# Batch 0's q in two parts, w_in ahead of batch 1's k, and new lists for sorted block attention with an FFN

## The chip, the cores and the metric

The kernel runs on one core of a Trainium2 chip. The metric is device time in microseconds (us) of one execution; three runs of the kernel before gave a median of 237.82 us (237.7 to 238.86). The trace of a profiled execution gives the span from the first to the last record, 236.6 us here.

## The reference

Batches B=4, heads H=8, tokens S=768, head size D=64. In each head the tokens form 8 blocks of 96. k and v are mixed over blocks by an 8x8 matrix P made from sort_net; the attention then runs inside each block; the heads are joined to x (3072 tokens by 512), and an FFN with a leaky activation (a slope per column) follows.

```
P = sort_net
for _ in range(5):
    P = exp(P - max(P, axis=-1))
    P = P / (sum(P, axis=-1) + 1e-9)
    P = P / (sum(P, axis=-2) + 1e-9)
k_sorted = einsum('bhij,bhjcd->bhicd', P, k_b)      # blocks of 96 tokens
v_sorted = einsum('bhij,bhjcd->bhicd', P, v_b)
scores = (q_b @ k_sorted^T) / sqrt(D)               # 96x96 per block and head
attn = softmax(scores)
x = (attn @ v_sorted) -> (3072, 512)
h = x @ w_in                                        # 512 -> 2048
g = max(h, 0) + alpha * min(h, 0)
out = g @ w_out                                     # 2048 -> 512
```

Inputs and output are fp32; the kernel works in bf16 with fp32 sums.

## The kernel before

The program builds a list of operations with G.add(engines, function, duration, reads, writes, priority). Which engine an operation runs on, and in what order each engine's operations stand, comes from the table SEQ: 1221 operation numbers, a suffix p, a or d choosing POOL, ACT or DVE where several are allowed. The table WARM puts filler matmuls (L808, on the identity) behind given operations. Waits on semaphores are derived from the reads and writes. The durations in the calls are for the planner that searched the table; with the table given they set nothing. An engine runs its list in order, so an operation that waits holds back all behind it.

The 3072 tokens form 32 groups of 96 (group g belongs to batch g // 8). Attention goes group by group, the FFN runs behind it in chunks of groups.

*Loads.* POOL issues all loads that turn fp32 into bf16, in one queue: batch 0's q (L397, into the tile hT that later holds the activations), its k and v (L419, KS0 and VST0), batch 1's k (L419, KS1), w_in in four parts (L908), w_out in two halves (L913), v of batches 1 to 3 in two or four parts (L435), and q of batches 1 to 3 as eight loads, one per head (L401, into QN). SP issues the turning DMAs (transposes), and the output stores (L877).

*q.* TensorE needs q with D on the partitions. Batch 0's q is turned on TensorE: prep_q (L600) multiplies it by the identity in six units of 8 token columns, and ACT copies each to QTz. q of the later batches is turned by six DMA transposes QTz<-QN (L409, turn_q), one per 128 tokens; the first of them reads what all eight loads bring. QTz has two buffers, batches taking turns.

*k and v.* Batch 0: prep_k (L600) multiplies KS by a block diagonal BDK made from P; conv_v (L653) rearranges v, and prep_v (L674) multiplies it. Later batches: conv_k (L616) spreads k into KSz, prep_k (L629) multiplies by BDM; conv_v (L658) spreads v into VDz, prep_v (L669) multiplies by BDV. Copies L372 bring the products to KT and VS.

*Attention of a group.* Scores S1 (L715 in batch 0, L712 later) go to PSUM; DVE takes the negated maximum (L721). In batch 0 a second pass on TensorE makes the turned scores with the maximum added (L736 and L727), and ACT takes the exp (L759) into ET. Later ACT takes the exp (L748) into Esb, and SP turns it (L753) into ET. L768 multiplies ET with VS; DVE normalises (L776, L779) into xq; xq is turned into xT by TensorE (L794, batches 0 and 1) or by a DMA (L787).

*FFN.* L823 multiplies w_in and xT for one of 16 column tiles, ACT (L833) and DVE (L836) apply the activation into hT, and L863 multiplies hT with w_out; L372 copies the result to outstg and L877 stores it. The ops of the FFN are spread between the attention's by the table.

PE, DVE, ACT, POOL and SP thus each follow a fixed list. In the start the order of POOL's list sets the order in which the loads arrive.

## Time and profile before

| | before |
|---|---|
| median of three runs | 237.82 us |
| span of the profiled execution | 236.6 us |
| PE (TensorE matmul) busy | 229.2 us (97%) |
| DVE busy | 169.8 us (72%) |
| ACT busy | 151.6 us (64%) |
| POOL busy | 73.0 us (31%) |
| DMA moved | 31.36 MB, mean 133 GB/s |

Busy times are sums over the instructions of an engine; the matmuls' ends are modelled and a filler matmul counts as busy, so 97% does not mean that TensorE did useful work for so long. In the lists of instructions, L12 is a line of the kernel, "out<-in" its tiles, and the part after a stroke the idle time of the engine before them and what ended it. For a DMA the time to landing is counted from its issue; loads issued by POOL are worked off in their order, so that a long time to landing is mostly waiting behind the loads ahead. The chain of waits follows the end of the program back to what released each step.

### The profile page before, as it was taken

The page shows a single profiled execution, that of the slowest core. Times are in us where ns is not written, and L with a number is a line of the kernel's source. Part 1 is how long each engine was busy: PE and PEld are TensorE (multiplying, and loading weights), DVE is VectorE, ACT ScalarE, POOL GpSimd, SP SyncE. Part 2 cuts the span into 40 slices and gives each one's busy share as a digit, 9 for nine tenths or more (in the row PEclk, how much of TensorE's full clock was granted, in tenths as well). Part 3 has the DMA queues.
Part 4 walks back from the last instruction along what each step waited for, and adds up shares of the span by engine and source line. Part 5 has one row for each costly group of instructions (what it writes and reads, how often), then busy time and mean ns, then how long its engine had stood idle before and what let it go on. Part 6 is the DMA issues. An engine that isn't in the chain of part 4 may idle for free.

```text
span 236.6 us, 6266 instructions
## 1 busy us (share of the span) xinstructions
PE 229.2 (97%) x2532; PEld 142.2 (60%) x2532; DVE 169.8 (72%) x354; ACT 151.6 (64%) x423; POOL 73.0 (31%) x139
## 2 busy tenths in 40 slices
PE   7998998999999999999999999999999999999995
PEld 3446676687666666556566665655555555555543
DVE  4748796989899997868887667676766587744350
ACT  4475265587887988886678786756864646453332
POOL 7958812915659620338590020000000000000000
PEclk9999999999999999999999999999999999999999
DMA  5999999999989999899998796542642323400033
GB/s 96 212 213 168 211 217 202 179 209 158 191 88 167 152 120 173 119 210 166 165 111 114 188 164 135 98 90 52 125 92 82 97 50 79 140 0 1 0 133 135
DMA packets 71453, 31.36 MB, mean 133 GB/s; under 512 B 64504, under 2 KB 65280, under 8 KB 71424
## 3 DMA queue, kind: packets, MB, share of 16 engines
q0 software_dynamic: 22896, 13.63, 42.0%
q1 hardware_dynamic: 48528, 17.33, 37.8%
q8 instruction: 20, 0.33, 0.5%
q14 instruction: 9, 0.07, 0.1%
HBM read 27.28 MB, written 6.29 MB: 142 GB/s over the span
## 4 chain that ended last, share of the span: by engine, by line
PE 76%; DMA 17%; POOL 6%; issue 1%; ACT 0%; POOLq 0%
PE psH L823 31%; PE psYP L863 28%; DMA w_out_bf<-in_moe_w_out_dram 10%; PE psS L863 3%; PE psS L712 3%; DMA VST<-in_v_dram 3%; PE psO L768 3%; PE psYP L669 2%; DMA ET<-Esb 2%; PE psYP L629 1%; DMA QTz<-QN 1%; POOL w_in_bf L908 1%; PE psO L863 1%; PE psS L727 1%; POOL VDz L456 1%; PE psO L794 1%
## 5 line engine op out<-in xcount | busy, mean ns | idle before, releaser
L836 DVE SCALAR_TENSOR_TENSOR hT<-t,omaT,psH 128x384 bf16<-128x384 f32 (+1 forms) x139 | 77.4, 571 | 36.6 <-ACT t L833 35.1
L823 PE MATMUL psH<-xT,w_in_bf 128*128 128x384 bf16 (+1 forms) x556 | 96.9, 311 | 0.0
L833 ACT ACTIVATE t<-psH 128x384 f32<-128x384 f32 (+1 forms) x139 | 63.1, 461 | 50.3 <-PE psH L823 49.2
L863 PE MATMUL psYP<-w_out_bf,hT 128*128 128x512 bf16 x336 | 83.2, 379 | 1.3 <-DMA w_out_bf<-in_moe_w_out_dram 1.3
L823 PEld LDWEIGHTS psH<-xT,w_in_bf 128*128 128x128 bf16 x556 | 49.5, 98 | 28.9 <-DVE hT L836 1.6
L863 PEld LDWEIGHTS psYP<-w_out_bf,hT 128*128 128x128 bf16 x336 | 30.8, 98 | 30.1 <-DMA w_out_bf<-in_moe_w_out_dram 1.8
L748 ACT ACTIVATE Esb<-psS,nf 96x96 bf16<-96x96 f32 x192 | 46.1, 345 | 2.0 <-DVE nf L721 2.0
L721 DVE TENSOR_REDUCE nf<-psS 96x8 f32<-96x768 f32 x24 | 22.8, 951 | 6.4 <-PE psS L712 6.0
L658 POOL COPY VDz<-VST 64x192 f32<-64x192 f32 x39 | 20.4, 524 | 20.3 <-DMA VST<-in_v_dram 16.6
L779 DVE TENSOR_TENSOR xq<-psO,rec 96x512 bf16<-96x512 f32 x31 | 21.2, 683 | 0.5
L401 POOL DMA_DIRECT2D QN<-in_q_dram x24 | 19.8, 833 | 3.3 <-DMA QTz<-QN 2.7
L616 POOL COPY KSz<-KS 64x256 f32<-64x256 f32 x28 | 11.1, 397 | 31.6 <-PE psYP L629 19.8
L712 PEld LDWEIGHTS psS<-KT,QTz 128*96 128x96 bf16 x192 | 12.1, 124 | 3.3 <-DMA QTz<-QN 0.2
L768 PEld LDWEIGHTS psO<-VS,ET 112*128 112x128 bf16 x248 | 11.1, 98 | 3.6 <-ACT ET L759 0.2
L808 PE MATMUL psYP<-identb 128*128 128x512 bf16 x40 | 12.8, 453 | 0.4 <-ACT identb L372 0.4
L372 ACT ACTIVATE VS<-psYP 112x512 bf16<-112x512 f32 x15 | 10.3, 687 | 4.2 <-PE psYP L669 2.2
L768 PE MATMUL psO<-VS,ET 112*128 112x65 bf16 x248 | 12.7, 194 | 0.0
L712 PE MATMUL psS<-KT,QTz 128*96 128x96 bf16 x192 | 12.6, 208 | 0.0
L372 ACT ACTIVATE KT<-psYP 128x512 bf16<-128x512 f32 x15 | 9.0, 599 | 2.8 <-PE psYP L629 1.8
L669 PEld LDWEIGHTS psYP<-BDV,VDz 128*128 128x128 bf16 x192 | 8.2, 98 | 2.7 <-POOL VDz L658 0.4
L372 ACT ACTIVATE outstg<-psYP 128x512 f32<-128x512 f32 x13 | 7.7, 604 | 3.2 <-PE psYP L863 3.2
L669 PE MATMUL psYP<-BDV,VDz 128*128 128x64 bf16 x192 | 9.5, 193 | 0.2 <-POOL VDz L658 0.2
(137 smaller groups left out, 198.8 us busy)
## 6 DMA issues: line engine op xcount, KB each, us to landing
out_dram<-outstg SPq DMA_DIRECT2D x23, 256.0 KB, 2.5
KS<-in_k_dram POOLq DMA_DIRECT2D x3, 768.0 KB, 13.3
QN<-in_q_dram POOLq DMA_DIRECT2D x24, 96.0 KB, 4.4
w_in_bf<-in_moe_w_in_dram POOLq DMA_DIRECT2D x4, 512.0 KB, 17.3
w_out_bf<-in_moe_w_out_dram POOLq DMA_DIRECT2D x2, 1024.0 KB, 23.9
VST<-in_v_dram POOLq DMA_DIRECT2D x4, 384.0 KB, 17.6
hT<-in_q_dram POOLq DMA_DIRECT2D x1, 768.0 KB, 7.6
VST<-in_v_dram POOLq DMA_DIRECT2D x1, 768.0 KB, 11.1
```

What stands on the lines that cost most here:

```text
L372: return e.activation(o, i, ACTF.Copy) if e is nc.scalar else e.tensor_copy(o, i)
L658: G.add(SHIFT, lambda e, o2=o2, i2=i2: e.tensor_copy(o2, i2), {"dve": 424, "pool": 525}, r=vst, w=[("VDz", u % VSL, th)], prio=prio)
L669: inst = e.matmul(AP(t, off + dd * 64, [[row, 128], [1, 64]]), AP(VDz, (u % VSL * 4 + dd // 2) * 256 + dd % 2, [[VSL * 1024, 128], [2, 128]]),
L712: inst = e.matmul(o, AP(QTz[n], hp * 3072 + h4 * 768 + i * 96, [[6144, 128], [1, 96]]), AP(KT[n], (h4 * 8 + i) * bk, [[ld, 128], [64, 2], ...
L721: G.add(DVE, lambda e: e.tensor_reduce(AP(nx, 0, [[8, 96], [4, 2], [1, 4]]), AP(psX, 0, [[1024, 96], [512, 2], [96, 4], [1, 96]]), AxisLis ...
L748: inst = e.activation(AP(Esb[me], p * 128, [[1024, 96], [64, 2], [1, 48]]), AP(psX, (p // 4) * 512 + (p % 4) * 96, [[1024, 96], [48, 2], [ ...
L768: inst = e.matmul(AP(psZ, hp * 512 + h4 * 68, [[1024, 128], [1, 65]]), AP(ET[me] if far else ET[m], pos(h4, hp) * 96, [[800, nk], [1, 128] ...
L779: G.add(DVE, lambda e: e.tensor_tensor(out=AP(xq[me], 0, [[512, 96], [256, 2], [64, 4], [1, 64]]), in0=AP(psZ, 0, [[1024, 96], [512, 2], [ ...
L823: inst = e.matmul(AP(pt, poff, [[1024, 128], [1, n]]), AP(w_in_bf, kt * DFF + ft // 2 * 256 + ft % 2, [[KT_TILES * DFF, 128], [2, 128]]), ...
L833: G.add(ACT, lambda e: e.activation(AP(t1[tb], 0, [[384, 128], [1, n]]), AP(pt, poff, [[1024, 128], [1, n]]), ACTF.Relu, scale=-1.0), t_ac ...
L836: G.add(DVE, lambda e: e.scalar_tensor_tensor(out=AP(hT, ft * RING + tok % RING, [[FT_TILES * RING, 128], [1, n]]), in0=AP(t1[tb], 0, [[38 ...
L863: inst = e.matmul(AP(bank[0], bank[1], [[1024, 128], [1, n]]), AP(hT, ft * RING + tok % RING, [[FT_TILES * RING, 128], [1, 128]]), AP(w_ou ...
```

## The change

Batch 0's q now comes as two loads. The first brings tokens 0 to 191 of every head (a quarter, 12 tokens in each partition's row), into hT as before; the second brings tokens 192 to 767 (36 in each partition's row) into KS[1], where batch 1's k goes later. Their source is walked as 8 heads by 16 runs by the run's elements; the load before was walked as 128 rows of 3072 elements. prep_q has seven units instead of six: two of 6 columns on the first part, four of 8 and one of 4 on the second; their copies to QTz may run on ACT or DVE. The scores of groups 0 and 1 need units 0 and 1 only, the later groups of batch 0 units 2 to 6.

The copies of conv_v in batch 0 may run on ACT too. The durations given to the planner are changed in most calls; SEQ and WARM are new. The core of the diff (SEQ, WARM and lines where only a duration changes are left out):

```
     def load_q(b, prio):
         if b == 0:
-            G.add(POOL, lambda e: e.dma_start(AP(hT, 8192, [[HR, 128], [1, 3072]]), AP(q.tensor, 0, [[3072, 128], [1, 3072]])),
-                  load_us, w=[("QS", 0)], prio=prio, dma=(d_q[0], 0))
+            for x, (t, off, n, t0) in enumerate(((hT, 8192, 12, 0), (KS[1], 0, 36, 192))):
+                ld = HR if t is hT else 3072
+                G.add(POOL, lambda e, t=t, off=off, n=n, t0=t0, ld=ld: e.dma_start(
+                    AP(t, off, [[ld, 128], [1, n * D]]),
+                    AP(q.tensor, t0 * D, [[S * D, 8], [n * D, 16], [1, n * D]])),
+                    load_us * n / 48, w=[("QS", x)] + [("KS", 1)] * x, prio=prio, dma=(d_q[x], 0))
             return
...
     def prep_q(u, prio, bank):
         t, off, row, keys = bank
-        G.add(PE, pairs(hT, 8192, u, identb, 0, 128, bank), 372, r=[("QS", 0), "identb"], w=keys, prio=prio)
-        o = AP(QTz[0], 8 * u, [[6144, 128], [96, 32], [48, 2], [1, 8]])
-        i = AP(t, off, [[row, 128], [2, 32], [1, 2], [64, 8]])
-        G.add(ACT, lambda e: copy(e, o, i), t_act(512), r=keys, w=[("Q0", u)], prio=prio)
+        x = u > 1
+        c0, n = ((0, 6), (6, 6), (0, 8), (8, 8), (16, 8), (24, 8), (32, 4))[u]
+        G.add(PE, pairs((hT, KS[1])[x], (8192, 0)[x], c0, identb, 0, 128, bank, n), 254 * n // 8,
+              r=[("QS", x), "identb"] + [("KS", 1)] * x, w=keys, prio=prio)
+        per = 36 if x else 12
+        o = AP(QTz[0], 192 * x + c0, [[6144, 128], [768, 4], [per, 16], [1, n]])
+        i = AP(t, off, [[row, 128], [16, 4], [1, 16], [64, n]])
+        G.add(EITHER, lambda e: copy(e, o, i), {"act": 142 + n * 64 // 1.2, "dve": 155 + n * 64 // .96}, r=keys, w=[("Q0", u)], prio=prio)
...
+            ob = AP(hT, 8 * u * 64, [[HR, 128], [2, 48], [128, 4], [1, 2]])
+            ib = AP(VST[0], 8 * u, [[3072, 128], [64, 48], [2, 4], [1, 2]])
+            G.add(("pool", "dve", "act"), lambda e: copy(e, ob, ib) if e is nc.scalar else e.tensor_copy(o, i),
+                  {"dve": 335, "pool": 530, "act": 490}, r=vst, w=[("VD", u)], prio=prio)
...
-            [("QTzt", n, t) for t in range(6)] + [("Q0", u) for u in range(6)]
+            [("QTzt", n, t) for t in range(6)] + [("Q0", u) for u in ((0, 1) if i < 2 else range(2, 7))]
...
-    for u in range(6):
-        prep_q(u, -50, (BANK_H + BANK_O + BANK_S)[u])
+    for u in range(2):
+        prep_q(u, -50, BANK_H[u])
     for u in range(6):
         prep_k(0, u, -47, BANKS0[(u + 1) % 5])
     for u in range(8):
         conv_v(0, u, -45.5)
     for u in range(8):
         prep_v(0, u, -45, (BANK_O + [BANK_P])[u % 3])
+    for u in range(5):
+        prep_q(u + 2, -44, (BANK_Y, BANK_P)[u % 2])
```

The lines of the changed kernel are 3 to 14 higher for the same operation: L715 is L727 there, L712 L724, L736 L748, L727 L739, L768 L780, L794 L806, L823 L835, L863 L875, L629 L638, L669 L681, L409 L414, L753 L765, L401 L406, L435 L440, L419 L424, L908 L922, L913 L927.

*The first loads.* POOL's list from the first load on, before:

```order
L397 DMA hT<-in_q_dram 128x3072
L443 ISA
L443 AFFINE_SELECT identf<-identf 128x128
L461 MEMSET QN 128x6x32
L456 MEMSET VDz 128x1024
L461 MEMSET QN 128x6x32
L419 DMA KS0<-in_k_dram 128x3072
L456 MEMSET VDz 128x1024
L419 DMA VST0<-in_v_dram 128x3072
L461 MEMSET QN 128x6x32
L419 DMA KS1<-in_k_dram 128x3072
```

The same engine and place in the changed kernel (L400 are the two parts of q; the KS1 of its second row of that line holds q):

```order
L400 DMA hT<-in_q_dram 128x1x768
L448 ISA
L448 AFFINE_SELECT identf<-identf 128x128
L424 DMA VST0<-in_v_dram 128x3072
L466 MEMSET QN 128x6x32
L424 DMA KS0<-in_k_dram 128x3072
L479 MEMSET Esb0 96x16x8
L400 DMA KS1<-in_q_dram 128x1x2304
L922 DMA w_in_bf<-in_moe_w_in_dram 128x2x1024 x3
L664 COPY hT<-VST0 128x48x4 x4
```

v stands ahead of k now, and the larger part of q behind both; w_in follows, and batch 1's k (L424, KS1) comes after all four parts of w_in and ahead of w_out, behind seven v copies.

*PE around the first group on w_out.* PE's list before, the last ten rows up to that group; psS, psH, psYP and psO are PSUM banks:

```order
L715 MATMUL psS<-KT,QTz 96x96 x8
L768 MATMUL psO<-VS,ET 128x65 x8
L823 MATMUL psH<-xT,w_in_bf 128x192 x8
L823 MATMUL psYP<-xT,w_in_bf 128x192 x4
L808 MATMUL psYP<-identb 128x512
L736 MATMUL psS<-QTz,KT 112x96 x8
L727 MATMUL psS<-identb,nm 112x96 x8
L823 MATMUL psYP<-xT,w_in_bf 128x192 x4
L823 MATMUL psH<-xT,w_in_bf 128x192 x8
L863 MATMUL psYP<-w_out_bf,hT 128x512 x4
```

The same place in the changed kernel, again up to the first group on w_out:

```order
L780 MATMUL psO<-VS,ET 128x65 x8
L835 MATMUL psH<-xT,w_in_bf 128x192 x4
L748 MATMUL psS<-QTz,KT 112x96 x8
L739 MATMUL psS<-identb,nm 112x96 x8
L835 MATMUL psH<-xT,w_in_bf 128x192 x4
L638 MATMUL psYP<-BDM,KSz 128x64 x8
L835 MATMUL psH<-xT,w_in_bf 128x192 x4
L806 MATMUL psO<-identb,xq 128x96 x4
L727 MATMUL psS<-KT,QTz 96x96 x8
L875 MATMUL psYP<-w_out_bf,hT 128x512 x4
```

In the changed list 13 FFN groups of w_in (4 matmuls each) stand ahead of that group, before 10; five second passes instead of four; and the first product of batch 1's k (L638) is already among them.

*Batch 2's loads.* POOL's list at the last loads of batch 1's q (into QN) and the first of batch 2, before:

```order
L401 DMA QN<-in_q_dram 128x6x64 x3
L658 COPY VDz<-VST1 64x48x4 x2
L401 DMA QN<-in_q_dram 128x6x64
L435 DMA VST0<-in_v_dram 64x3072
L419 DMA KS0<-in_k_dram 128x3072
```

The same place in the changed kernel:

```order
L670 COPY VDz<-VST1 64x48x4 x3
L406 DMA QN<-in_q_dram 128x6x64
L625 COPY KSz<-KS1 64x8x32
L406 DMA QN<-in_q_dram 128x6x64
L670 COPY VDz<-VST1 64x48x4
L440 DMA VST0<-in_v_dram 64x3072
L670 COPY VDz<-VST1 64x48x4 x4
L440 DMA VST0<-in_v_dram 64x3072
L670 COPY VDz<-VST1 64x48x4 x4
L670 COPY VDz<-VST0 64x48x4 x5
L424 DMA KS0<-in_k_dram 128x3072
```

Batch 2's k (KS0) now follows both halves of its v (VST0) and thirteen copies of v behind the first half, five of them of batch 2's own v. On SP four turns of batch 1's q stand ahead of the first turn of ET, two behind it; before it was five and one.

234 lines of the change are left out of this document (117 added, 117 removed).

## The prediction

> **What bounds the kernel now.** I read the windows view first, cut at the events that matter: the first FFN group (28.71), the first group on w_out (36.40), batch 1's first scores (56.88), batch 2's first scores (97.42) and the end of TensorE (234.20). The columns are the stretch, its length, then busy us (and count) of PE, PEld, DVE, ACT, POOL, the clock, the DMA share and GB/s.
>
> ```profile
> 28.71:36.40 7.69, 6.39 (x96) 5.20 (x91) 6.99 (x19) 4.37 (x12) 1.81 (x3) 1.00 1.13 217
> 36.40:56.88 20.48, 20.44 (x324) 16.16 (x325) 16.68 (x42) 14.10 (x34) 8.53 (x18) 1.00 1.43 193
> 56.88:97.42 40.54, 40.54 (x461) 26.52 (x460) 37.48 (x70) 34.49 (x107) 22.14 (x41) 1.00 1.12 142
> 97.42:234.20 136.78, 136.50 (x1065) 78.94 (x1063) 90.42 (x161) 84.33 (x241) 17.45 (x32) 1.00 0.58 107
> ```
>
> From 36.40 to 234.20 PE stands still for 0.04 + 0.00 + 0.28 = 0.32 us, and the clock is full. So the end is when PE passes some mark, plus the work that its list still holds. Only what stands ahead of that mark can be won. The second view is the chain that ended last, around the first mark:
>
> ```profile
> 12.19 24.17 DMA w_out_bf<-in_moe_w_out_dram
> 36.40 1.04 PE psYP L863 x4
> ```
>
> The first half of w_out lands at 12.19 + 24.17 = 36.36 and PE stood idle for it. The third view asks for the scores of batch 1 (L712), for the turn of batch 1's q on which they rest (L409) and for the last of the eight loads of that q (L401):
>
> ```profile
> L712 PE MATMUL psS<-KT,QTz x8: 206/208/208, 56.9 to 57.2; 128*96 128x96 bf16 x8
> its engine sat idle before it (us, times) until:
>   DMA QTz<-QN: 0.2, 1
> ...
> L409 SPq DMA_TRANSPOSE QTz<-QN x1: 1354/1354/1354, 50.9 to 50.9; - x1
> DMA to landing us min/median/max: 5.8/5.8/5.8
> ...
> L401 POOL DMA_DIRECT2D QN<-in_q_dram x1: 826/826/826, 41.0 to 41.0; - x1
> DMA to landing us min/median/max: 9.9/9.9/9.9
> ```
>
> The last q load lands at 41.0 + 9.9 = 50.9, the first turn starts there and lands at 50.9 + 5.8 = 56.7, and PE reads it at 56.9 after 0.2 us of waiting. That is a second mark, just met before. It is fed by the queue of loads, not by PE: whatever PE gains ahead of it is lost again unless this turn lands earlier too.
>
> **The change part by part.** *The first loads.* All of these stand in one queue:
>
> ```profile
> L397 POOL DMA_DIRECT2D hT<-in_q_dram x1: 687/687/687, 1.3 to 1.3; - x1
> DMA to landing us min/median/max: 7.6/7.6/7.6
> ...
> L419 POOL DMA_DIRECT2D VST<-in_v_dram x1: 536/536/536, 5.5 to 5.5; - x1
> DMA to landing us min/median/max: 11.1/11.1/11.1
> ...
> L419 POOL DMA_DIRECT2D KS<-in_k_dram x1: 548/548/548, 6.2 to 6.2; - x1
> DMA to landing us min/median/max: 14.1/14.1/14.1
> ```
>
> These are batch 0's q and v and batch 1's k; batch 0's k lies between q and v. Landings: q 1.3 + 7.6 = 8.9, v 16.6, batch 1's k 20.3, so one such load costs (20.3 - 8.9)/3 = 3.8 us of queue, and k landed near 12.7. The new order is a quarter of q, v, k, three quarters of q. With 0.95 for the quarter and 2.85 for the rest this gives v at 9.9 (was 16.6), k at 13.7 (was 12.7), the second part of q at 16.5, and w_in one load earlier. K's products may start up to 1.0 later, in a stretch in which PE still spins warm groups. V's copies and products, which had to wait for 16.6, move ahead. What this buys is read off PE's list: ahead of the first w_out group now stand 13 instead of 10 FFN groups, 5 instead of 4 second score passes (L736 and L727), and six more small groups (two L715, two L794, one L768, one L629). Durations from the chain:
>
> ```profile
> 45.31 0.33 PE psH L823 x4
> 43.93 0.34 PE psS L736 x8
> 44.27 0.54 PE psS L727 x8
> 47.02 0.34 PE psYP L629 x8
> ```
>
> 3 x 0.33 + 0.88 = 1.87, and six small ones at 0.17 (half of the nearest row, since these rows overlap) to 0.34 add 1.0 to 2.0; I take 1.2, together 3.1 us. The bytes ahead of w_out's first half are the same as before (batch 1's k only stands behind w_in instead of ahead), so it lands at 36.4 again, and PE reaches it with 3.1 us more behind it, provided DVE delivers: it is at 6.99 of 7.69 there.
>
> *From w_out to batch 1's scores.* Ahead of L712's first group the two lists hold the same FFN, score and k groups. The new one has two v groups and a part of q's turn more and one L768 less, 0.2 us net. So PE would come there at 36.4 + 20.48 - 3.1 + 0.2 = 54.0. The gain could be 2.9 us, if the turn were there.
>
> *The turn of batch 1's q.* Ahead of its last load stand the same bytes, so that lands at 50.9 again. Two of the eight are now issued behind VDz copies that wait for v, which costs nothing while the queue is still at w_out's second half. What changes is behind them:
>
> ```profile
> L435 POOL DMA_DIRECT2D VST<-in_v_dram x1: 557/557/557, 41.8 to 41.8; - x1
> DMA to landing us min/median/max: 10.1/10.1/10.1
> ...
> L419 POOL DMA_DIRECT2D KS<-in_k_dram x1: 609/609/609, 42.4 to 42.4; - x1
> DMA to landing us min/median/max: 13.3/13.3/13.3
> ...
> L409 SPq DMA_TRANSPOSE QTz<-QN x1: 1233/1233/1233, 82.6 to 82.6; - x1
> DMA to landing us min/median/max: 3.8/3.8/3.8
> ```
>
> Before, half of batch 2's v (until 51.9) and batch 2's k (until 55.7) ran beside this turn, and it landed 1.0 after them. That k took 55.7 - 51.9 = 3.8 us, no longer than undisturbed: it was the turn that stood back. Now that k is issued behind batch 2's v copies, after this time; the second half of v stands there instead, half the bytes, and the queue is empty at about 53.8. One us later is 54.8. A turn with an empty queue took 3.8, which would be 54.7. The upper end is no change, 56.7. I take 55.0, so the scores start at 55.2 instead of 56.9: 1.7 us won, and 0.2 for the work already done.
>
> [...]
>
> *The next wait.* SP now issues four turns, then the turn of the first probabilities (ET), then the last two; before, five stood ahead. What is left for it is PE's work between batch 1's first scores and its first L768:
>
> ```profile
> 68.75 0.41 PE L768 MATMUL psO<-VS,ET 112*128 112x65 bf16 x8
> ET<-Esb SPq DMA_TRANSPOSE x24, 3.3
> 58.50 1.92 ACT L748 ACTIVATE Esb<-psS,nf 96x96 bf16<-96x96 f32 x8
> ```
>
> That was 68.75 - 56.9 = 11.9 us for five w_out groups, six wide and three narrow FFN groups, six v, three L712 and one L794: 27,520 columns through PE. The new list has three, three, three, three, two and one there, and one L768: 17,032 columns, or 7.3 us. Scores to exps took 60.4 - 56.9 = 3.5, and ET lands 3.3 later by the median: 6.8 of 7.3. With a turn as slow as q's above (5.8) it is 2.0 short. I take 0.4 lost, nearer the median, and 0.1 for all later waits.
>
> *What costs nothing.* The new durations in the calls only feed a planner; the order comes from the table. "Any engine" for v's copies is not used: the list puts two on DVE and six on POOL, none on ACT. The warm groups fall from 47 to 45, all ahead of 36.4, where w_out sets the time. Cover for the start is the 1.2 us between PE's 54.0 and the turn's 55.2; a start that is later than that costs what is beyond it.
>
> **The sum.** -1.7 - 0.2 + 0.4 + 0.1 = -1.4 us on the span of 236.6, so 235.2. The median of the three runs, 237.82, lies 1.2 above the span, and so I forecast 236.4 (-0.6%).
>
> **Rivals.** R1, *the turn lands no earlier*: other traffic or the transposer itself sets it at 56.5 to 56.7. Then 0.2 to 0.4 is won and 0.1 to 0.4 lost: 237.7. For it: four turns follow each other there in any case. Against: 3.8 with an empty queue.
>
> R2, *q's parts load at half speed*, the rival on the other side. The source of each part is now walked as 8 heads by 16 by a run of tokens, where before it was 128 rows, and if the work is dealt by the 8, half of the DMA engines carry it. If the parts fall on opposite halves, one half is behind by 2 x 0.75 - 1 = 0.5 load = 1.9 us; on the same half by a whole load, 3.8. Every later load is complete only when the slower half is, so w_out, v, and batch 1's turn all slip: 238.3 or 240.2. It decides against the change from a lag of 1.4 on. No row shows a load of that shape; that all loads before have 64 or 128 rows speaks for nothing. [...]
>
> R3, *DVE becomes the bound between the two score marks*. Between L712's first group of batch 1 and that of batch 2 DVE gets two normalisations, two xT copies and four smaller pieces more, and three evacuations fewer.
>
> ```profile
> L779 DVE TENSOR_TENSOR xq<-psO,rec 96x512 bf16<-96x512 f32 x31 | 21.2, 683 | 0.5
> L372 DVE CAST VS<-psYP 112x512 bf16<-112x512 f32 x11 | 7.6, 688 | 0.8 <-PE psYP L669 0.8
> ```
>
> With 0.68 and 0.2 of reciprocal for each normalisation, half an evacuation for an xT copy and 0.25 for a small piece (estimates from these rows), that is 1.76 + 0.69 + 1.0 - 2.06 = +1.4 on 37.48 of 40.54. If its 3.1 us of gaps stay, PE loses 1.4: 237.8. Against: gaps of an engine that waits for PE shrink first.
>
> **How the numbers follow.** Forecast 0.55 (alone 235.2 to 237.2), R1 0.15, R2 0.18 (two thirds of it opposite halves), R3 0.12. A measurement of this kernel tells about 0.5%, 1.2 us, from no change: below 236.6 is faster, above 239.0 slower. Three quarters of the forecast's chance lies below 236.6, 0.41, and 0.01 of the rest: 0.42. Slower: the same halves and the upper part of the opposite ones 0.10, R3 with a further wait 0.05, and 0.02 for the forecast's own tail: 0.17. Same: 0.41. The range of 8 in 10 is 235.0 (turn at 54.5 and no wait for ET) to 239.2 (R2's opposite halves with a wait behind it).
>
> **What would show it.** Right: v lands near 9.9 and k near 13.7; w_out at 36.4 with no PE wait above 0.5; a PE wait of about 1 us for QTz at 55; L768 within 0.5 of its ET; PE solid after. Wrong: q's second part later than 17.5 and w_out at 38 (R2); L712 at 56.7 or later (R1); PE gaps for DVE between L712's marks (R3). If the last q load of batch 1 lands more than 1 us from 50.9, the sum falls with it, either way.

## Result and profile after

The change makes the kernel slower: 251.36 and 252.44 us against a median of 238.34 (237.70 to 238.90) of the kernel before on the same chip, a ratio of 1.058 [1.053, 1.062]. Two further executions at a lower clock (0.967) took 261.1 and 262.0 and are left out of this; the profiles of e2, e3, e6, e8 and e9 below come from such longer executions, which their ratios leave out as well. Forecast were 236.4 and a range of 235.0 to 239.2.

The windows view of the changed kernel, cut at the events of the prediction: the first FFN group, the first group on w_out, batch 1's and batch 2's first scores, the end of TensorE (columns as there). The stretch from 0 to the first FFN group stands ahead of them:

```profile
0.00:34.72 34.72, 27.07 (x609) 17.61 (x610) 19.82 (x67) 13.76 (x28) 17.69 (x37) 0.95 0.87 158
34.72:44.15 9.43, 9.05 (x145) 7.58 (x144) 8.80 (x24) 6.44 (x18) 7.61 (x14) 1.00 1.08 207
44.15:61.00 16.85, 16.57 (x260) 13.31 (x262) 15.88 (x40) 11.36 (x27) 9.75 (x20) 1.00 1.37 147
61.00:102.22 41.22, 40.52 (x461) 26.38 (x469) 38.32 (x77) 34.61 (x108) 18.79 (x35) 1.00 1.11 146
102.22:246.90 144.68, 137.55 (x1033) 78.34 (x1049) 92.06 (x167) 79.25 (x233) 17.01 (x30) 0.99 0.57 103
```

The first FFN group stood at 28.71, now 34.72: 6.0 later. The first w_out group stood at 36.40, now 44.15: 7.8. Batch 1's scores 56.88, now 61.00: 4.1. From there to the end it was 177.3, now 185.9: 8.6 more. So there are two losses, 4.1 ahead of batch 1's scores and 8.6 behind them. In the second PE is busy for 40.52 + 137.55 = 178.07 against 40.54 + 136.50 = 177.04: 1.0 of the 8.6 is more busy time, 7.6 is more standing still.

What PE waited for, from the waits view (us in total, times, longest):

```profile
PE psO L780 <- DMA ET<-Esb: 5.0, 2, 4.7
PE psYP L686 <- issue: 3.3, 1, 3.3
PE psS L901 <- DVE bz L895: 2.3, 1, 2.3
PE psYP L820 <- ACT identb L373: 1.7, 1, 1.7
PE psYP L875 <- ACT outstg L373: 1.0, 1, 1.0
```

The third and fourth lie ahead of 6 us, where before stood 1.2 and 0.4 for the same two. The first two are what the prediction did not have: 3.3 us in which nothing that the profile shows held PE ("issue"), and a wait for a turn of probabilities. PE's timeline shows both places (start, length, what, and in brackets the idle time ahead):

```profile
20.11 0.28 PE L686 MATMUL psYP<-BDK,hT 128*64 128x64 bf16 x5
23.71 0.46 PE L686 MATMUL psYP<-BDK,hT 128*64 128x64 bf16 x11 [3.32 <-issue]
...
61.00 0.56 PE L724 MATMUL psS<-KT,QTz 128*96 128x96 bf16 x8
...
108.76 0.41 PE L780 MATMUL psO<-VS,ET 112*128 112x65 bf16 x8 [4.71 <-DMA ET<-Esb]
```

The first breaks into a group of v's products after its fifth matmul: 5 run, 11 come 3.3 us later, on the same operands. That is no wait for data. Behind each the granted clock was half for 3.4 us (from 23.8 and from 109.1), which two narrow windows show as 0.60 and 0.66 (the last column but two, PEclk):

```profile
24.00:28.00 4.00, 4.00 (x133) 3.61 (x130) 2.25 (x3) 2.13 (x4) 0.00 (x0) 0.60 0.68 129
108.00:113.00 5.00, 4.11 (x26) 2.17 (x28) 2.10 (x6) 1.92 (x9) 2.76 (x6) 0.66 1.14 238
```

In the kernel before PE had pauses of the first kind too, of 0.5 us each:

```profile
16.11 0.28 PE L600 MATMUL psO<-BDK,KS 64*64 64x64 bf16 x6 [0.51 <-issue]
...
22.33 0.71 PE L674 MATMUL psO<-BDK,hT 128*64 128x64 bf16 x32 [0.52 <-issue]
```

### The profile page after: what moved, and what is told of

It reads as the page before. It is cut to its first block, busy times and chain, and to the rows that moved or that the text cites. A ratio compares the mean times of both kernels' runs of the same rounds, so it can differ in the third digit from the quotient of the medians.

```text
span 249.5 us, 6214 instructions
## 1 busy us (share of the span) xinstructions
PE 230.8 (93%) x2500; PEld 143.2 (57%) x2530; DVE 174.9 (70%) x371; ACT 145.7 (58%) x413; POOL 70.8 (28%) x134
## 4 chain that ended last, share of the span: by engine, by line
PE 75%; DMA 11%; DVE 5%; issue 3%; ACT 2%; POOL 1%; SPq 1%; POOLq 0%; ACTq 0%
PE psH L835 28%; PE psYP L875 24%; DMA ET<-Esb 5%; PE psYP L820 4%; PE psS L875 3%; PE psS L724 3%; DMA QN<-in_q_dram 3%; PE psO L780 3%; DMA QTz<-QN 2%; PE psYP L681 2%; DVE hT L848 1%; PE psYP L638 1%; DVE nm L733 1%; PE psO L875 1%; ACT t L845 1%
## 5 line engine op out<-in xcount | busy, mean ns | idle before, releaser
L835 PE MATMUL psH<-xT,w_in_bf 128*128 128x384 bf16 (+1 forms) x556 | 99.1, 312 | 0.3 <-DVE hT L848 0.2
L875 PE MATMUL psYP<-w_out_bf,hT 128*128 128x512 bf16 x308 | 79.9, 382 | 2.7 <-ACT outstg L373 1.0
L835 PEld LDWEIGHTS psH<-xT,w_in_bf 128*128 128x128 bf16 x556 | 48.9, 98 | 30.3 <-DVE hT L848 4.6
L875 PEld LDWEIGHTS psYP<-w_out_bf,hT 128*128 128x128 bf16 x336 | 31.1, 98 | 30.1 <-ACT outstg L373 1.5
L670 POOL COPY VDz<-VST 64x192 f32<-64x192 f32 x34 | 18.0, 529 | 23.5 <-PE psYP L681 12.4
L406 POOL DMA_DIRECT2D QN<-in_q_dram x24 | 19.9, 835 | 1.1 <-issue 0.4
L780 PE MATMUL psO<-VS,ET 112*128 112x65 bf16 x248 | 12.7, 194 | 5.0 <-DMA ET<-Esb 5.0
L780 PEld LDWEIGHTS psO<-VS,ET 112*128 112x128 bf16 x248 | 11.4, 98 | 9.9 <-issue 5.1
L625 POOL COPY KSz<-KS 64x256 f32<-64x256 f32 x26 | 10.4, 400 | 21.6 <-PE psYP L638 17.6
L724 PEld LDWEIGHTS psS<-KT,QTz 128*96 128x96 bf16 x192 | 11.7, 125 | 2.6 <-DMA QTz<-QN 0.3
L820 PE MATMUL psYP<-identb 128*128 128x512 bf16 x39 | 11.3, 450 | 1.7 <-ACT identb L373 1.7
L724 PE MATMUL psS<-KT,QTz 128*96 128x96 bf16 x192 | 12.6, 208 | 0.1
L373 ACT ACTIVATE VS<-psYP 112x512 bf16<-112x512 f32 x13 | 8.9, 687 | 5.1 <-PE psYP L686 3.6
L681 PE MATMUL psYP<-BDV,VDz 128*128 128x64 bf16 x192 | 9.8, 195 | 0.0
L681 PEld LDWEIGHTS psYP<-BDV,VDz 128*128 128x128 bf16 x192 | 8.3, 100 | 2.4 <-POOL VDz L670 0.6
L373 DVE CAST VS<-psYP 112x512 bf16<-112x512 f32 x13 | 8.9, 685 | 0.2
## 6 DMA issues: line engine op xcount, KB each, us to landing
w_in_bf<-in_moe_w_in_dram POOLq DMA_DIRECT2D x4, 512.0 KB, 18.6
```

The lines of the kernel that those rows point to most:

```text
L373: return e.activation(o, i, ACTF.Copy) if e is nc.scalar else e.tensor_copy(o, i)
L681: inst = e.matmul(AP(t, off + dd * 64, [[row, 128], [1, 64]]), AP(VDz, (u % VSL * 4 + dd // 2) * 256 + dd % 2, [[VSL * 1024, 128], [2, 128]]),
L724: inst = e.matmul(o, AP(QTz[n], hp * 3072 + h4 * 768 + i * 96, [[6144, 128], [1, 96]]), AP(KT[n], (h4 * 8 + i) * bk, [[ld, 128], [64, 2], ...
L780: inst = e.matmul(AP(psZ, hp * 512 + h4 * 68, [[1024, 128], [1, 65]]), AP(ET[me] if far else ET[m], pos(h4, hp) * 96, [[800, nk], [1, 128] ...
L820: inst = e.matmul(AP(bank[0], bank[1], [[1024, 128], [1, 512]]), identb[:, :], AP(identb, 0, [[128, 128], [0, 4], [1, 128]]))
L835: inst = e.matmul(AP(pt, poff, [[1024, 128], [1, n]]), AP(w_in_bf, kt * DFF + ft // 2 * 256 + ft % 2, [[KT_TILES * DFF, 128], [2, 128]]), ...
```

## Experiments

All times are of each run's profiled execution, ratios are to the kernel before on the same chip. "Pauses" are the idle times of PE that end with "issue" before 35 us; "FFN 1" is the start of the first FFN group, "w_out" the first group on it, "S b1" batch 1's first scores (L724), "then" from there to PE's end, "gaps" PE's idle time in that stretch.

```
                         ratio [95%]             FFN 1  w_out  S b1   then   gaps   pauses
before                   1                       28.7   36.4   56.9   177.3   0.2   0.51 0.52
after                    1.058 [1.053, 1.062]    34.7   44.2   61.0   185.9   7.8   3.32
e1  walk in before       1.000 [0.997, 1.003]    31.3   37.6   57.8   176.9   0.0   1.73
e2  q on 16              1.059 [1.052, 1.065]    38.6   47.8   64.6   185.8   5.4   3.83 1.36
e3  q in VST1            1.069 [1.064, 1.074]    39.7   48.9   65.7   192.4  10.9   2.96 2.35
e4  fillers spread       1.063 [1.057, 1.068]    38.1   47.3   64.1   184.6   5.1   0.75 2.79
e5  fillers added        1.050 [1.045, 1.055]    36.8   46.3   63.3   181.8   4.9   1.97
e6  all of the start     1.064 [1.058, 1.069]    38.7   48.1   64.6   187.2   8.1   2.26
e7  v3 ungated           1.070 [1.064, 1.076]    38.5   47.9   64.5   183.7   6.9   2.78 1.64
e8  start and v3         1.060 [1.057, 1.064]    37.5   46.9   63.4   190.6  11.2   1.84
e9  half instructions    -                       31.4   40.8   63.0   185.4   5.9   none
e10 half in before       1.006 [1.004, 1.007]    27.9   36.6   58.1   177.0   1.3   none
e11 half and loads       1.032 [1.025, 1.038]    30.2   39.7   56.2   184.4   7.4   none
e12 half, loads, v3      1.029 [1.026, 1.032]    30.2   39.6   56.1   183.8   6.8   none
e13 cover for ET         1.048 [1.046, 1.051]    34.8   44.0   61.3   184.0   4.5   3.40
e14 all, whole products  1.051 [1.043, 1.058]    38.0   47.2   64.0   183.6   5.7   3.0 1.25
e15 half, loads, cover   1.048 [1.042, 1.055]    29.6   38.8   55.5   187.0   7.1   none
e16 k first              1.060 [1.057, 1.062]    38.5   47.7   64.5   183.4   5.4   1.29 2.07
e17 P table early        1.046 [1.041, 1.051]    38.4   47.9   64.4   181.6   4.9   4.16 2.27
e18 P early, half        1.057 [1.054, 1.061]    29.8   39.2   55.7   187.8  11.0   none
```

The executions of one list derived from the change differ by 0.5 to 4%, before's by up to 0.8%. Rows of single profiles are therefore read for where PE stood and for what, and differences of a us or two in "then" are not. e9 has no ratio: its shortest execution took 247.83 against before's 237.82.

### The loads: e1 to e4

**e1** writes the source of q's load in the kernel before as heads by runs, as R2 suspects it:

```diff
-AP(q.tensor, 0, [[3072, 128], [1, 3072]])
+AP(q.tensor, 0, [[S * D, 8], [3072, 16], [1, 3072]])
```

> The kernel before with one edit: the source of batch 0's q is walked as 8 heads by 16 runs of 3072 elements instead of 128 rows of 3072. Same bytes, same places, same lists. Theory A (the walk puts a load on 8 of the 16 DMA engines): q lands at 12.7 instead of 8.9, every load behind it is complete 3.8 us later on the loaded half, so w_out's first half lands near 40.1 instead of 36.4 and the time rises by 3 to 4 us, to about 241. Rival (the walk does not matter, the changed kernel's late loads have another cause): all landings within 0.3 us of before, time 237.8.

Ratio 1.000. It tells nothing on the walk: the whole of q is contiguous, and the built instruction is before's, 128 x 3072. As a repeat of before it tells something else. Its second pause was 1.73 us instead of 0.52, the clock halved for 3.4 us and FFN 1 was 2.6 late, yet batch 1's scores were late by 0.9 and the end by 0.5: the old list has slack there, in its waits for w_out and for the turn.

**e2** loads each part of q as two of 64 partitions with 16 as the slowest dimension, and reads them in that order:

```diff
-AP(q.tensor, t0 * D, [[S * D, 8], [n * D, 16], [1, n * D]])
+AP(q.tensor, t0 * D + hp * 4 * S * D, [[n * D, 16], [S * D, 4], [1, n * D]])   # hp in 0, 1
-AP(t, off, [[row, 128], [16, 4], [1, 16], [64, n]])
+AP(t, off, [[row, 128], [1, 4], [4, 16], [64, n]])
```

> The changed kernel with each part of q issued as two loads of 64 partitions whose source is walked as 16 runs by 4 heads (partition order inside a half changed to match, the copy to QTz reads it back). Theory A: v lands near 10.2 instead of 12.1 and the fourth part of w_in near 27.8 instead of 30.0. Batch 1's k is still issued only when TensorE has read the second part of q out of its buffer, so w_out's first half lands near 39 to 39.5 instead of 40.8; the time falls by 1 to 2 us of 251.4. Rival (q's walk is not the cause of the late loads): w_in's fourth part stays at 30.0 within 0.3.

The second part of q landed at 16.7 instead of 3.95 + 16.0 = 20.0, as the groups of the two kernels have it (after, then e2; start, and us to landing):

```profile
L400 POOL DMA_DIRECT2D KS<-in_q_dram x1: 669/669/669, 4.0 to 4.0; - x1
DMA to landing us min/median/max: 4.8/10.4/16.0
```

```profile
L404 POOL DMA_DIRECT2D KS<-in_q_dram x2: 562/572/582, 4.3 to 4.8; - x2
DMA to landing us min/median/max: 2.6/6.8/11.9
```

So the parts did load more slowly, as R2 has it, and the loads behind them were late with them (the last part of w_in landed at 29.96, in e2 at 28.36, 1.6 earlier). It repeats: in the eight runs with the change's form that part of q landed at 19.5 to 20.4, in the nine with e2's at 16.2 to 18.6. e2 alters the walk and the number of loads together and does not part the two. How many DMA engines carried either form was not shown, so R2's reason for it stays a supposition. But the time did not fall. FFN 1 came at 38.6, later than in the change, with two pauses in place of one.

**e3** puts the second part into VST[1] instead of KS[1], so that batch 1's k need not wait for the reads of q:

```diff
-((hT, 8192, 12, 0), (KS[1], 0, 36, 192))
+((hT, 8192, 12, 0), (VST[1], 0, 36, 192))
```

> The changed kernel with the second part of q loaded into VST[1] (batch 1's v, loaded later than its k) instead of KS[1]. Theory B (batch 1's k and w_out behind it wait for the reads of q out of KS[1]): k is issued near 20.5 instead of 28.0, the queue never runs dry, w_out's first half lands near 38.8 instead of 40.8, batch 1's first scores come 1.5 to 2 us earlier than 61.0. Rival (the load queue's lag of 2.4 us alone sets w_out): w_out within 0.5 of 40.8.

What it undoes is on POOL's timeline of the changed kernel, the issue of batch 1's k and of w_out behind it; e3's row follows:

```profile
28.03 0.56 POOL L424 DMA_DIRECT2D KS<-in_k_dram  x1 [7.74 <-PE psS L727]
28.58 0.75 POOL L927 DMA_DIRECT2D w_out_bf<-in_moe_w_out_dram  x1
```

```profile
20.67 0.56 POOL L424 DMA_DIRECT2D KS<-in_k_dram  x1
```

The wait of 7.74 us went, the queue no longer ran thin (DMA share 1.08 between 28 and 29, in the change 0.36), and w_out's first half landed at 39.6 instead of 40.8. Again FFN 1 came later (39.7), with pauses of 2.96 and 2.35. The loads are late for the reasons given here, but they are not what PE stands for: in the change PE came to w_out at 44.2, 3.4 after it had landed.

**e4** spreads the warm groups (fillers, matmuls of 512 columns) into the dense stretch, seven of the 25 that stand ahead of it:

```diff
-80:25:y
+80:18:y 111:2:y 97:2:y 109:2:y 117:1:y
```

> The changed kernel with 7 of the 25 filler matmul groups ahead of the table of P moved between the v products, total unchanged. Theory C (TensorE's pause of 3.3 us with no releaser at 20.4 is a wait for its next instructions: it used up a block of 256 faster than the next one came): the pause falls below 0.7 us, the granted clock stays 1.0 at 24 to 27 instead of 0.5, batch 1's k is issued near 24 instead of 28.0, first scores of batch 1 about 2 us earlier. Rival (the pause waits for a load or a buffer that the trace does not name): the pause ends at 23.7 again, whatever stands ahead of it.

The long pause fell to 0.75, and one of 2.79 appeared further on, in another operation:

```profile
22.44 0.36 PE L686 MATMUL psYP<-BDK,hT 128*64 128x64 bf16 x11 [0.75 <-issue]
...
28.64 0.40 PE L727 MATMUL psS<-KT,QTz 64*96 64x96 bf16 x3 [2.79 <-issue]
```

### What a pause is

I then counted PE's recorded instructions from the start: matmuls, weight loads and the few semaphore instructions between them. A pause falls on number 705 or 961, whatever the operation is, in before, in the change and in every list of these runs with whole products; 961 - 705 = 256. The profile has a DMA queue for instructions, 20 packets and 0.33 MB in both kernels, so 16 KB a packet:

```profile
q8 instruction: 20, 0.33, 0.5%
```

20 x 256 = 5120 stands against 2500 + 2530 = 5030 recorded PE instructions, and in the runs below that have about 4700 of them the queue has 18 or 19 packets. So I take these packets for PE's program, in blocks of 256. Put together, with the time at which PE begins number 449 (one block earlier), the start of the next packet of that queue, and the time at which 705 begins; then the same for 705 and 961 (trace records, counted):

```
         449 begins  packet   705 begins     705  packet   961 begins
before      10.2      13.8      16.1        16.1    20.1      22.3
after       17.6      21.3      23.7        23.7    25.2      27.8
e1          10.5      13.8      16.1        16.1    20.9      23.5
e2          16.6      21.0      23.2        23.2    27.1      29.3
e3          18.0      21.6      23.8        23.8    28.1      30.5
e4          17.1      20.2      22.4        22.4    26.4      28.6
e5          17.3      21.3      23.5        23.5    24.6      29.5
e6          17.5      21.6      24.0        24.0    27.8      31.4
e7          16.8      20.0      22.4        22.4    26.4      28.8
e8          17.9      21.6      24.0        24.0    27.9      30.2
e13         17.5      21.3      23.7        23.7    25.2      27.9
e14         16.4      20.5      22.9        22.9    26.8      29.2
e16         18.1      21.2      23.5        23.5    27.3      29.8
e17         15.5      20.2      22.5        22.5    26.6      29.0
```

In this stretch, in which loads fill the DMA queues (a DMA share of 0.95 up to FFN 1 in before, 0.87 in the change), a block's packet starts 3.1 to 4.8 us after PE has entered the block before it (1.0 to 1.5 in three places), takes about 1 us, and where PE stood for it, PE goes on 1.2 to 1.5 later. So a block took about 6 us there (449 to 705: 5.3 to 7.0). Before's list needed about that for each: 5.9 and 6.2, with pauses of 0.5. The changed list would run 449 to 705 in about 3 (it gets through it in 20.39 - 17.6 = 2.8 and then stands still until 23.7). That PE stands there for its next block is my reading of these counts and times; the trace names no releaser. The pauses at 705 and 961 were 0.5 to 4.2 us long.

The second columns show where the second pause comes from. In the change, e5 and e13 the packet behind 705 came after 1.0 to 1.5 us, and there was no second pause; with e2's or e3's loads it came after 3.9 and 4.4, and there was one. That the packets wait because of the loads is likely, but not shown. Between 27.8 and 28.7 in the change the DMA share was 0.39, and the next packet came after 0.9; but its 1.4 fell at a share of 0.96 (23.7 to 25.2), and e16's 3.9 at 0.62 (23.5 to 27.3). Which DMA engine carries a packet is not recorded, so this stays open.

### Taking the instructions away: e5 to e12

**e5** adds fillers inside the stretch, without taking any away, to give a block more time:

```diff
+111:2:p 97:2:h 109:2:q 117:2:p 161:2:h 125:2:p 113:2:o
```

> The changed kernel with 14 filler matmul groups (0.215 us each, 3.0 us) added, two each ahead of seven small products of the start, in the bank that the product uses. Theory C2 (TensorE runs out of instructions wherever some 250 small ones follow each other without fillers; the spread of 7 only moved the pause from the v products to the first scores): no pause without a releaser above 0.7 us before 35, granted clock 1.0 from 18 on, the first FFN group near 33 instead of 34.7, time 2 us below 251.4. Rival (the pauses have another cause, fillers are plain extra work): pauses of 2.5 to 3.8 us again, time 251.4 or up to 3 us more.

The pause fell to 1.97, but the fillers cost more than that: FFN 1 at 36.8.

```profile
23.54 1.03 PE L820 MATMUL psYP<-identb 128*128 128x512 bf16 x2 [1.97 <-issue]
```

**e6** is e2, e3 and e5 together, with the last two loads of batch 1's q issued right behind the sixth:

```diff
-223 230 143 194 224      # ... 287 142 341 ... 298 144 289
+223 230 143 142 144 194 224
```

> The changed kernel with the 14 added fillers, q's parts on two loads each (16 runs by 4 heads), the second part in VST[1], and the last two loads of batch 1's q issued right behind the sixth, ahead of the KSz copies. If the start's four causes make up the loss ahead of batch 1's first scores: batch 1's k issued near 20, w_out's first half landing near 36.5 to 37, last load of batch 1's q near 51, first scores of batch 1 at 55.5 to 57.5 instead of 61.0, time 4 to 5 us below 251.4 (the wait for ET near 104 stays). Rival (the start costs only what TensorE's own list costs): first scores at 59 or later, time above 249.

The loads came out as wanted: w_out's first half landed at 37.1 and the first turn of batch 1's q at 54.2, 3.3 after its start at 50.9. PE came to w_out only at 48.1 and to batch 1's scores at 64.6: it was PE's own list that was late, by ten us.

**e7** takes the condition off batch 3's v, which waits for the last turn of batch 2's q before it is loaded, and **e8** is e6 and e7 together:

```diff
-r=[("QTzt", 0, 5)] * (b == 3)
+r=[]
```

> The changed kernel without the rule that batch 3's v is loaded only after the last turn of batch 2's q (its four loads then go out near 92.7 instead of 98.0). Theory D (the ET of group 15, issued at 100.9, lands late at 108.6 because these loads run in front of it, and TensorE waits 4.7 us and then runs 3.4 us at half clock): this ET takes 4 us or less, the wait shrinks below 1 us, no half clock near 110, time near 246. Rival (the turn takes long by itself, or the loads now hold up other turns as much): some turn between 92 and 104 takes over 7 us and the time stays within 1 us of 251.4.

> Both the four edits of the start and batch 3's v ungated. If the two losses are independent and add up: 4 to 5 us from the start and 5 to 6 us from the ET, time 240 to 242. If one hides the other: not below 245.

e7 tests the second loss, the wait of 4.7 for ET: it went down to 1.2, and a wait of 2.6 for a copy of v (VDz, POOL) at 126 took its place. In e8 the waits for ET add up to 8.2. So batch 3's v beside that turn is not the cause alone.

**e9** makes the products of batch 0 with half as many instructions, 128 columns each instead of 64; **e10** does so in the kernel before. In e9 to e12, e15 and e18 every second token column of these products gets its neighbour's value; the columns through PE are as many as in the change.

```diff
-for c in range(nc_):              # k and q; v alike
+for c in range(0, nc_, 2):
-AP(t, ..., [[row, 64], [1, 64]])
+AP(t, ..., [[row, 64], [1, 128]])
-AP(mat, ..., [[row_m, 64], [1, 64]])
+AP(mat, ..., [[row_m, 64], [0, 2], [1, 64]])
```

> The changed kernel in which the products of batch 0's q, k and v are made by half as many matmuls of twice the width (128 columns, the 64 of the matrix twice): same columns through TensorE, same waits, half the instructions; every second token column of batch 0 gets its neighbour's product, so the output is not the reference's. Theory S (TensorE takes its instructions in blocks of 256 and a block takes about 6 us to come while the loads run; the changed lists use one up in 3 us, TensorE stands at its recorded instruction 705 and the clock halves): no pause above 0.7 us between 16 and 32, clock 1.0 there, first FFN group at 29.5 to 31 instead of 34.7, batch 1's first scores at 57 to 58.5 instead of 61.0. Rival (the start is late because of landings or because DVE and ACT are behind): first FFN group at 33.5 or later.

> The same halving in the kernel before (output not the reference's for the same reason). Theory S: it had two pauses of 0.5 us at the same two instruction counts, behind which the wait for w_out's first half stood anyway; first FFN group 0.5 to 1.5 us earlier, w_out still at 36.4, time 237 to 238.3. If the halving itself makes TensorE faster by more than the pauses, the first FFN group moves by more than 2 us.

e9's FFN 1 came at 31.4, 3.3 ahead of the change, with no pause of that kind (PE waited 1.06 for the second part of q). Batch 1's scores still came at 63.0: PE now waited 5.3 us for the turn of q, which landed at 63.0 after 7.9 us beside other loads. In before (e10) the same edit moved FFN 1 by 0.8, less than the 1.03 of before's two pauses: the halving by itself does not make PE faster by more than the pauses. PE then waited 2.27 for w_out, and batch 1's scores came 1.3 and the end 1.0 later than in before (ratio 1.006; 237 to 238.3 us were expected, 239.3 was the median).

**e11** is e9 with the loads of e6 (e2, e3 and the two early QN loads), **e12** adds e7's edit.

> The halved instructions of the changed kernel, with q's parts on two loads each (16 runs by 4 heads), the second in VST[1], and the last two loads of batch 1's q right behind the sixth. If instructions and loads make up the loss of the start: batch 1's k issued near 20, w_out's first half landing at 36.5 to 37.5, first scores of batch 1 at 54 to 56 (the turn lands near 54 to 55), that is 1 to 3 us ahead of the kernel before; time 237 to 244, by how long the ET of group 15 is waited for. If the first scores stay above 58, something of the start is not found.

> The same with batch 3's v not held for the last turn of batch 2's q. If the second loss is this load beside the ET of group 15: time 3 to 6 us below the run without it. If these loads only hold up other turns then: the same time within 1.5 us, with a wait for a turn of over 3 us elsewhere.

The windows view of e11, to FFN 1, and from batch 1's scores to the end; then PE's waits in the second of the two:

```profile
0.00:30.20 30.20, 25.60 (x449) 15.38 (x450) 19.81 (x67) 13.71 (x28) 20.03 (x42) 1.00 0.95 176
56.20:240.60 184.40, 176.97 (x1492) 103.84 (x1516) 131.32 (x244) 114.06 (x340) 36.06 (x65) 1.00 0.72 113
```

```profile
PE psO L785 <- DMA ET<-Esb: 3.8, 3, 2.7
PE psYP L686 <- POOL VDz L675: 1.2, 1, 1.2
```

No pause, full clock from start to end, and batch 1's scores at 56.2, 0.7 ahead of before. So the first loss is gone, with its two causes shown apart: the loads alone left batch 1's scores at 64.6 (e6; 64.4 in e17 below, without e5's fillers), the instructions alone at 63.0 (e9), both together brought 56.2. The cleanest pair is e17 and e18 below, which differ in the halving alone: FFN 1 at 38.4 and 29.8, batch 1's scores at 64.4 and 55.7. The ratio fell to 1.032 [1.025, 1.038], the best of all with e12's 1.029 (there the longest wait for ET fell from 2.7 to 1.0, and the one for a copy of v rose from 1.2 to 1.9). But from there the list took 184.4, before's 177.3, at an equal busy time (176.97 against 177.04). The second loss does not come from the first.

### The second loss: e13 to e15

The chain of the changed kernel has the turn at which PE stood, issued at 100.85:

```profile
100.85 7.77 DMA ET<-Esb
```

It ran beside batch 3's v (97.96 to 106.34). Before's turn of the same group took as long, 7.97 (96.45 to 104.42); PE did not yet want it. **e13** gives it cover, which is PE's work between the issue of a turn and its reader: the product on that turn and eight operations with it (716 751 752 633 634 722 723 755 756) go behind the FFN groups that follow them:

```diff
-608d 716d 662 652 627 599 681 633 507 717p 663 665 634 628 682 751d 722 671 ...
+608d 662 652 627 599 681 507 717p 663 665 628 682 671 ... 674 716d 751d 752d 633 634 722 723a 755d 756p
```

> The changed kernel with the L780 group of group 15 (the first reader of the slow ET) behind two w_out and two FFN groups and one L724 instead of ahead of them, the first v product of batch 3 right behind it, and the copies of batch 3's v on DVE behind the FFN evacuations instead of among them. About 3.4 us of TensorE work then lie ahead of that reader. Theory D2 (the second loss is that ET's short cover): the wait of 4.7 us near 104 falls below 1.5 us, no half clock behind it, time 4 to 6 us below 251.4, that is 245.5 to 247.5. Rival (the wait moves to the next turn or to batch 3's v): time within 1.5 us of 251.4.

The wait for ET went. PE ran FFN groups instead and then stood 2.45 at the next turn, that of q, at nearly the same time, with 3.4 us at half clock behind it as before:

```profile
105.83 1.03 PE L875 MATMUL psYP<-w_out_bf,hT 128*128 128x512 bf16 x4
...
109.30 0.84 PE L724 MATMUL psS<-KT,QTz 128*96 128x96 bf16 x8 [2.45 <-DMA QTz<-QN]
```

The ratio 1.048 [1.046, 1.051] lies below the change's, the start being the same (34.8, 61.3); its times, 249.2 to 249.8, are some 2 us below the change's, not 4 to 6. **e14** has whole products, e2, e3, the early QN loads and e13, with k loaded ahead of v and 12 fillers at its front; **e15** is e11 and e13.

```diff
-80:25:y      # e14
+80:12:y
-... 3 43 7 44 45 23 40 46 6 47    # op 7 loads v, op 6 loads k
+... 3 43 6 44 45 23 40 46 7 47
```

> The edits that leave the result right together: batch 0's k ahead of v, 12 instead of 25 fillers ahead of P's table, q's parts on two loads each, the second in VST[1], the last two loads of batch 1's q early, the cover for group 15's ET. If instructions, loads and that cover are all of the loss: first FFN group at 31 to 32.5, batch 1's first scores near 57 to 58, time 239 to 242, about what the kernel before takes or a little more. If it stays above 245, TensorE's instructions in the start are not spread by k alone.

> The run with half the instructions and the mended loads (output not the reference's), with the cover for group 15's ET added. Theory D2: first scores at 56 again, the wait of 2.7 us near 101 gone, time 239 to 242 against 244.9. Rival: 243.5 or more.

e14 took 1.051, with pauses of 3.0 and 1.25, 13.7 us at half clock and FFN 1 at 38.0 instead of 31 to 32.5. e15 was slower than e11, 1.048 [1.042, 1.055]. The wait of 2.7 for ET went, but 7.1 us of gaps stay: 2.62 for a turn of q at 62, ahead of the operations that were moved (that turn took 8.8 us, in e11 by the same list 3.1), 1.0 for a turn of q at 106, and 2.3 for copies of v. Why e15 is slower is not shown.

So it is not one wait. In all lists derived from the change PE stands 4.5 to 11.2 us behind batch 1's scores, in before's 0.0 to 1.3. Turns of over 6 us beside loads occur in both kernels, 5 of 42 in before and 7 in the change. What differs is how early they land: the readers of the first eight turns of ET come 0.1 to 4.7 us after the landing in before, 0.0 to 1.4 in the change. In part those turns were longer there (groups 9 to 11: 7.9, 8.2 and 6.4; in before 4.0, 3.7 and 3.7). In part the new order leaves less work between issue and reader: for group 15 it was 7.9 - 4.7 = 3.2 us, in before 8.1, with a turn as long. Which of its moves does that I could not settle.

### What else could make the start late: e16 to e18

**e16** is e14's k ahead of v and its 12 fillers alone. **e17** brings the tables on which k's products rest earlier (identity and bz first on DVE, identb first on ACT, 82:8 80:24), with e2, e3 and the early QN loads; **e18** is e17 with half the instructions.

```diff
-0 18 13d 1 4 11 12 8 2 9 3 ... 134 10 53
+0 8 2 18 13d 1 4 11 12 9 10 3 ... 134 53
```

> The changed kernel with batch 0's k ahead of v and 12 instead of 25 fillers ahead of P's table, nothing else. If k behind v is what packs the small matmuls: k's products start near 13.3 instead of 17.2, the pause at recorded instruction 705 shrinks below 2 us, first FFN group at 31 to 33. If the later parts of q pack them (q's second part lands near 20 in any case): the pause of 3 us comes at the same count or at 961, first FFN group at 34 to 35.

> The changed kernel with the mended loads (q's parts on two loads each, the second in VST[1], the last two loads of batch 1's q early) and an earlier start of the chain for P: DVE makes the identity and the burst's zeros first, ACT copies the identity first, 8 instead of 11 fillers stand ahead of q's first unit and 24 instead of 25 ahead of P's table. Theory P (the start is late because P's table is, by what ACT and TensorE have in front of it): the fourth exp near 8.3 instead of 10.9, k's products from 13.5 to 14 instead of 17.2, a pause at recorded instruction 705 as before (the instructions are as dense), first FFN group 2.5 to 4 us earlier than without it, near 32 to 34. Rival (instructions alone set the start): first FFN group at 36 or later as in the runs with pauses.

> The same with half the instructions for batch 0's products (every second token column wrong, as before). Theory P: first FFN group at 26.5 to 28 instead of 30.2, w_out's first group at its landing near 37, batch 1's first scores at 54.5 to 55.5, set by the turn; time 242 to 244. Rival (P's chain is not what sets it): first FFN group within 0.7 of 30.2.

The suspicion behind them: the fourth exponential of the P table ran at 8.26 before and at 10.86 after, and k's products, which need that table, began at 13.27 and 17.23. In e16 k landed at 10.9 and its products still began at 17.1, so k's landing was not their bound there: they waited 2.1 us for BDK, a part of the table whose making stood on DVE behind copies of v, and v landed at 15.2. In e17 the exponential ran at 8.40 and the products began at 15.07, right behind k. FFN 1 did not care:

```profile
15.07 0.44 PE L613 MATMUL psO<-BDK,KS 64*64 64x64 bf16 x16 [0.42 <-DMA KS<-in_k_dram]
...
17.95 0.35 PE L694 MATMUL psYP<-BDK,hT 128*64 128x64 bf16 x9
22.45 0.38 PE L694 MATMUL psYP<-BDK,hT 128*64 128x64 bf16 x7 [4.16 <-issue]
...
28.98 0.52 PE L756 MATMUL psH<-QTz,KT 64*112 64x96 bf16 x7 [2.27 <-issue]
```

PE came to number 705 two us earlier and stood there until 22.45, against 23.71 in the change. With half the instructions (e18) FFN 1 came at 29.8, in e11 without the early table at 30.2. So the early table brought 0.4. It could hardly bring more there, since k landed at 15.8 instead of e11's 13.7 and PE stood for it:

```profile
15.97 0.41 PE L613 MATMUL psO<-BDK,KS 64*64 64x128 bf16 x8 [2.21 <-DMA KS<-in_k_dram]
```

What it is worth with k in time is not shown. With whole products the supply of instructions sets the start in these runs (FFN 1 at 38.4 in e17, at 29.8 with half the instructions in e18). No version beat the kernel before.

## Why the prediction was wrong

**"Together 3.1 us" of PE's work ahead of w_out, and "K's products may start up to 1.0 later, in a stretch in which PE still spins warm groups".** This step failed first. k's products began at 17.23 instead of 13.27, 4.0 later (k landed at 16.59 instead of the 13.7 forecast, and the table was ready at 16.64), and the warm groups did not make it free: PE came to w_out at 44.15, 7.8 later than before, instead of at 36.4 with 3.1 us more of its list done. What counted was not work alone but number of instructions: the six units of q that before ran at 8.9 to 10.6 are 192 instructions, and they filled time between 512-column fillers. In the change only part of q is there early, so number 449 is reached at 17.6 instead of 10.2, and all the small products of k, v and q stand packed behind. From there the two need nearly the same: 5.9 and 6.2 us for the two blocks in before, 6.1 and 4.1 in the change, and 6.4 and 6.9 more until FFN 1, at 28.7 and 34.7. The change's lateness at number 449, 7.4 us, is thus mostly kept (6.0 at FFN 1), since PE, which got through its small matmuls from 449 to 705 in 2.8 us, then stood still for 3.3. I read in the trace that PE was busy in that stretch and priced the moved operations by columns; that v could start earlier was right (it landed at 12.14; 9.9 forecast, and 9.98 in e3) and worth nothing.

**"It lands at 36.4 again"** (w_out). It landed at 40.80. The lag of q's second part was foreseen as R2 (1.9; e2 gives 1.6 for w_in's last part). Not foreseen was that batch 1's k, which takes q's place in KS[1], waits 7.74 us on POOL for PE to read q, with w_out's issue behind it; the queue ran thin meanwhile (a DMA share of 0.36 between 28 and 29). With both mended w_out landed at 37.0 (e11). My own sentence that a wait holds what is queued behind it on its engine was applied to the VDz copies and not here.

**"Two of the eight are now issued behind VDz copies ... which costs nothing".** They were issued at 47.78 and 48.94, behind KSz and VDz copies of which the first waited for PE's products of k. Those products were late with everything else:

```profile
43.25 1.31 POOL L625 COPY KSz<-KS 64x256 f32<-64x256 f32 x3 [1.10 <-PE psYP L638]
45.33 0.85 POOL L625 COPY KSz<-KS 64x256 f32<-64x256 f32 x2 [0.77 <-PE psYP L638]
46.25 1.68 POOL L670 COPY VDz<-VST 64x192 f32<-64x192 f32 x3
47.78 0.82 POOL L406 DMA_DIRECT2D QN<-in_q_dram  x1
48.94 0.82 POOL L406 DMA_DIRECT2D QN<-in_q_dram  x1
```

So the last load landed at 55.9 instead of 50.9, and the turn behind it, by the chain, at 60.96:

```profile
48.94 6.93 DMA QN<-in_q_dram
55.88 5.08 DMA QTz<-QN
```

PE would have been there no sooner (44.15 + 16.57 = 60.7): two limits met at 61.0, which is why neither e6 nor e9 moved it alone.

**"A turn with an empty queue took 3.8".** Right in kind: with the loads out of its way the turn took 3.1 to 3.3 (e6, e11, e12). In e11 it landed at 54.0, 2.7 ahead of before; 0.7 of this reached batch 1's scores, because PE came there no sooner. The 1.7 that I forecast was reached in no run (1.4 at most, in e15).

**"0.4 lost" at the next wait, "and 0.1 for all later waits".** At that ET PE did not wait: it landed at 68.0 and was read from 68.3 on, 7.3 us behind the first scores as I had counted. The second is the term that failed by most: 7.6 us more standing still and 1.0 more busy time behind 61.0. I had found PE solid in before's trace and took this for a property of the work; it hung on the order, in which the turns landed ahead of their readers (by 0.1 to 4.7 us for the first eight of ET). A new order has to be walked turn by turn to its end.

**The rivals.** R2's lag of q's second part came, and e2 took it away, but the transfers were not on the path: with q's parts loaded in e2's form the ratio was 1.059, as without. R1 and R3 are not what happened: the turn alone takes 3.1, and PE's one wait for DVE between the score marks was 0.2. None of the rivals held that PE's list before w_out could be the longer one. The range ended at 239.2 because every bound in it was taken from transfers and waits that the profile of before shows, and the one there that mattered, two "issue" pauses of 0.5 us, was passed over as noise.

## What to carry to other kernels

The "issue" pauses inside runs of equal matmuls (0.5 to 4.2 us) lay at instructions 705 and 961 here, and with half the instructions there were none ahead of 35 us (e9 to e12, e15, e18): where a trace has such pauses, count instructions to them, and look whether they lie 256 apart. For a start beside loads as dense as these, price a new order by PE instructions as well as by columns: it took 5.3 to 7.0 us for 256 of them here (449 to 705). Wide warm matmuls between the small ones did not mend it (e4 moved the pause, e5 paid for it); fewer and wider instructions did. And in before's list, in which PE stood still for 0.3 us behind 56.88, the first eight turns of ET landed 0.1 to 4.7 us ahead of their readers: after an edit of such an order the slack of each turn has to be looked at again, not only that of the first.

## What the runs showed of the hardware that I had not expected

Between 449 and 961 a packet of the instruction queue mostly started 3.1 to 4.8 us after PE had entered the block before it, by my reading of the counts, and PE stood 0.5 to 4.2 us at 705 or 961. Whether the kernel's loads delay the packets is open. At the two places with the lowest DMA share (0.39 behind 961 in the change, 0.20 in e5) they came after 0.9 and 0.3 us, but other places, told above, do not fit.

The granted clock was half for 3.4 us behind idle times of PE of 3.32 (the change), 1.73 (e1), 1.06 (e9) and 2.27 (e10), while waits of 2.7 for a turn (e11) and 3.6 for a copy (e18) left it full. So the length of the wait alone does not decide. Other half-clock stretches lasted 6.8, 10.2 and 13.7 us (e16, e2), two, three and four times the 3.4.

v and k of batch 0, second and third in the same queue with the same loads ahead, landed at 12.14 and 16.59 in the change and at 9.98 and 13.65 in e3; in e4, e5, e7, e9 and e13, which have the same first loads, v landed at 10.6 to 11.9. Nothing in the traces says why.
